# Weight sums on GpSimd in steps of 128 columns, and two blocks of attention outputs half a position later, in a fused attention and gated feed-forward kernel

## The chip, the cores and the metric

The kernel runs on one core of a Trainium2 chip. The metric is the device time of one execution in microseconds (us): before the change the median of three runs is 1006.04 us (1006.01 to 1006.66). Engines are named as in the profile: PE is TensorE, with PEld its weight loads; DVE is VectorE, ACT is ScalarE, POOL is GpSimd, and SP the queue that issues the DMAs.

## The reference

Windowed causal attention over 8 batches, 8 heads, 576 positions and head width 64, followed by a gated feed-forward layer over all 4608 tokens:

```
scores = q @ k.T / sqrt(64), kept where 0 <= i - j < 64
attn   = softmax(scores);  x = attn @ v, as (4608, 512)
gate   = sigmoid(x @ w_gate)          # 512 x 1536
val    = x @ w_val                    # 512 x 1536
out    = (gate * val) @ w_out         # 1536 x 512
```

q, k and v are float32; the three weight matrices come as float64 and are converted on the chip.

## The kernel before, in words

**Tiles.** The tokens are cut into twelve tiles of 384 (TT). The attention of a tile is done in four units (t, p), p being a pair of heads. The feed-forward layer runs over pairs of tiles, s = 0 to 5. Every product of full precision is made from a high and a low part of each operand: x_hi w_hi + x_lo w_hi + x_hi w_lo. A tile "hi" is a rounded copy made by ACT or DVE, and "lo" is the difference, made by DVE or POOL (split, line 145).

**A unit** goes through stages. stage_a or stage_s (lines 194, 263) makes the scores on PE (L208) into two PSUM banks and the softmax: DVE adds the mask and finds the minimum (L232), ACT takes the exponential and its sum (L241), DVE inverts the sums (L249, L250), and DVE or POOL multiplies by the inverse (L259). stage_b (line 285) transposes the probabilities on PE (L290), and ACT copies each half to SBUF as pT (L295). stage_c (line 300) multiplies by v on PE (outputs, L319), into a bank oo, and ACT copies it to xf (L307). From the third tile on, scores, transposes and outputs all take their banks from one pool of two (a_bank, line 191), in turn: two for the scores, two for the transposes, one for the outputs. The second bank of a unit's scores is therefore the one that the outputs of the unit before held.

**The first pair** (s = 0) uses plain products, up (L349) and down (L419), while weights are still being converted: conv_a on ACT (L112, L113), conv_b on DVE (L121 to L125), conv_c on ACT and DVE (L146, L147), with stores and loads on SP. The attention of the second pair's tiles (the third and fourth tile) runs in between.

**The later pairs** use a scheme of Strassen's kind: seven products in place of eight (product, L568, in PRODUCTS order), for each of k = 0 to 5 and for gate and value (m = 0, 1). It needs sums of quarters of the weights, S1 to S4. These sums are made once, during the first two pairs, twelve sets (m, k) in all, and stored to DRAM for the pairs behind. The functions are:

- sums_load (line 477) loads the two weight blocks a1 and a2.
- sums_make (line 492) makes four sums of 128x256 on POOL (L496 to L499) in a tile sw.
- sums_split (line 502) takes the hi part of two sums at once, 128x512, on ACT (L146), and the lo part on POOL (L147), in tiles ws.
- sums_store (line 514) stores the parts on SP (L471), one DMA for each sum.

In the second pair DVE combines the products from PSUM (u and c, L574; the copy p, L580), multiplies by the gate (h, L608; hb, L613), and makes hl (L388). PE's next product into a bank waits for these readers.

**Order.** Every step is put at a time in planner units (put, line 623), and the events are traced in order of time. PE's instructions keep exactly that order (pe, line 83). The order on the other engines is dealt by the framework's scheduler, which plays the program through with its own instruction times. The plan of the first pair is a list: items up (0, j), down (0, j-1), up (1, j) for j = 0 to 11. Line 661 says at which positions of that list the stages a, b and c of the eight units of the third and fourth tile stand. A whole number is ahead of that item; a half is between the gate product and the value product of an up item (attend, line 666). Units go in the order of unit(1, n), so that n = 0 and 1 are the first two units of the third tile.

Of the kernel before, what the change touches and what calls it, by code (L numbers as in the profile page):

```python
# [9 lines left out]
F32 = mybir.dt.float32  # L10
# [8 lines left out]
P = 128  # L19
# [7 lines left out]
def attn_ffn(ctx: ExitStack, tc: tile.TileContext, qT, kT, vN, w_gate, w_val, w_out, out):  # L27
# [3 lines left out]
    nc = tc.nc  # L31
# [95 lines left out]
    def conv_c(i):  # L127
        j, m = divmod(i, KINDS)
        _, w32 = conv.pop(i)
        H = DM // 2  # L130
        tag, bufs = ("W", WB) if m < 2 else (f"wo_{j}", 1)
        w2 = wts.tile([P, 2, 2, H], F32R, name=f"w{m}_{j}", tag=tag, bufs=bufs)
        if m == 2:
# [11 lines left out]
    def split(w32, hi, lo, eng):  # L145
        cp = nc.scalar.copy(hi, w32)  # L146
        eng.tensor_sub(out=lo, in0=w32, in1=hi.bitcast(F32))  # L147
        return cp.ins
# [341 lines left out]
        sums[m, k] = aa  # L490

    def sums_make(m, k):
        H = DM // 2
        a1, a2 = sums[m, k]
        sw = mp.tile([P, 4, H], F32, name=f"sw_{m}_{k}", tag="raw", bufs=RAW)
        nc.gpsimd.tensor_add(out=sw[:, 0, :], in0=a2[:, :H], in1=a2[:, H:])  # L496
        nc.gpsimd.tensor_sub(out=sw[:, 1, :], in0=sw[:, 0, :], in1=a1[:, :H])
        nc.gpsimd.tensor_sub(out=sw[:, 2, :], in0=a1[:, :H], in1=a2[:, :H])
        nc.gpsimd.tensor_sub(out=sw[:, 3, :], in0=a1[:, H:], in1=sw[:, 1, :])  # L499
        sums[m, k] = sw  # L500

    def sums_split(m, k):

        H = DM // 2
        sw, sums[m, k] = sums[m, k], []
        for i in range(0, 4, 2):
            w2 = wts.tile([P, 2, 2, H], F32R, name=f"ws{i}_{m}_{k}", tag="W", bufs=WB)
            split(sw[:, i:i + 2, :], w2[:, :, 0, :], w2[:, :, 1, :], nc.gpsimd)
            sums[m, k].append(w2)
            for e in range(2):  # L510
                n = [w for w, _, _ in PRODUCTS].index(f"S{i + e + 1}")
                wt[(1, k, m, n)] = w2[:, e]
# [136 lines left out]
    def unit(s, n):  # L649
        return 2 * s + n // 2 % 2, n // 4 + n % 2 * 2  # L650
# [7 lines left out]
        if n < NF:  # L658
            plan.append(("up", 1, n))
    at, now = {}, 0.0  # L660
    for n, at_plan in enumerate(((4.5, 8, 8.5), (9, 12, 13), (13.5, 16, 17), (17.5, 20.5, 22),
                                 (22.5, 25, 26), (26.5, 30, 31), (31.5, 35, 36), (36.5, 40, 41))):
        for f, x in enumerate(at_plan):
            fill.setdefault(x, []).append((f, *unit(1, n)))
# [64 lines left out]
    for s in range(1, NS):  # L729
# [17 lines left out]
        for k in range(NK):  # L747
            if s == 1:
                for m in range(2):
                    for d, f in ((-6, sums_load), (0, sums_make), (7, sums_split), (11, sums_store)):  # L750
                        put(now - (21 if k else 38) + 13 * m + d, 7, f, m, k)
                for x, d in enumerate((-18, -14, -5)):
                    put(now + d, 7.5, a_load, s, k, x)
            else:
                for q in range(NPR):
                    put(now - 24 + 3 * q, 7.5, w_load, s, k, q)
            for m in range(2):
                for n in range(NPR):
                    put(now, 9, product, s, k, m, n)
                    now += PRT  # L760
                    if n in (2, 4, 6) and len(downs) > (RESERVE if m else 0) * (k == 1):
                        j, x = downs.pop(0)
                        put(now, 9, down, a, j, x, j == 0, False)
                        now += DPT
                    attend(slot)
                    slot += 1
            downs += [(j, x) for j in (k, k + NK) for x in range(TB)]
# [65 lines left out]
```

## Time and profile before

| | |
|---|---|
| median of 3 runs | 1006.04 us |
| the profiled execution's own time | 1005.49 us |
| its span | 1003.2 us |
| granted PE clock, mean | 0.998 |
| PE busy | 978.2 us (98%) |
| DVE, ACT, POOL busy | 641.8, 530.8, 231.5 us |

The span is the time from the first instruction to the last in one execution that the hardware profiler took; the 2.3 us more in that execution's own time lie around it. Busy times count instructions of the engine, without queue waits. In lists of instructions, the first number is the start in us from the span's start and the second the duration; what stands in brackets is the engine's idle time just ahead and the instruction that ended it. In lists of waits, the numbers are us in total, times, and the longest. In lists by tile, they are the minimum, median and maximum of the duration in ns. In groups by line, they are busy us, mean ns of one, and idle us ahead.

### The profile page before, as it was taken

How to read it: one execution, taken by the hardware profiler on the slowest of the kernel's cores; microseconds unless marked ns; L12 is line 12 of the kernel's file. 1: busy time of each engine (PE TensorE's matmuls, PEld its weight loads, DVE VectorE, ACT ScalarE, POOL GpSimd, SP SyncE). 2: the span in 40 equal slices, each digit the busy share in tenths (PEclk: the TensorE clock that was granted, in tenths of full speed). 3: DMA queues.
4: the chain of work that ended last, by engine and by line, in shares of the span. 5: the costliest groups of instructions: out<-in, count | busy, mean ns of one | idle time of the engine just before them, and what ended most of it. 6: DMA issues, size and time to landing. Idle time of an engine off the chain costs nothing.

```text
span 1003.2 us, 19702 instructions
## 1 busy us (share of the span) xinstructions
PE 978.2 (98%) x6984; PEld 881.6 (88%) x6984; DVE 641.8 (64%) x1737; ACT 530.8 (53%) x1433; POOL 231.5 (23%) x240
## 2 busy tenths in 40 slices
PE   6999999999999999999999999999999999999998
PEld 5888999889888889999988999988999988999996
DVE  7899888636766665666675666575666667344532
ACT  7887878544655745545554555464564464211122
POOL 4200122225454031212141121213212124010100
PEclk9999999999999999999999999999999999999999
DMA  9999888469875625767643776751776661566500
GB/s 345 315 340 363 319 287 274 157 233 298 256 246 187 219 77 177 246 207 227 216 136 97 236 235 203 224 184 45 241 236 215 202 184 71 159 214 204 189 32 32
DMA packets 84337, 208.91 MB, mean 208 GB/s; under 512 B 9360, under 2 KB 24976, under 8 KB 84240
## 3 DMA queue, kind: packets, MB, share of 16 engines
q1 hardware_dynamic: 84240, 207.66, 63.0%
q8 instruction: 56, 0.92, 0.4%
q14 instruction: 41, 0.34, 0.1%
HBM read 165.94 MB, written 41.68 MB: 207 GB/s over the span
## 4 chain that ended last, share of the span: by engine, by line
PE 64%; ACT 4%; DVE 1%; issue 0%; DVEq 0%; ACTq 0%
PE pr L568 35%; PE y L419 23%; PE s L208 2%; ACT p L241 2%; PE pp L290 2%; PE s L319 1%; ACT g L362 1%; ACT e L361 0%; PE pr L319 0%; PE oo L319 0%; DVE u L574 0%; ACT L241 0%; DVE rs L249 0%; DVE c L574 0%; DVE g L366 0%
## 5 line engine op out<-in xcount | busy, mean ns | idle before, releaser
L419 PE MATMUL y<-w,hh 128*128 128x512 f32 x804 | 250.3, 392 | 0.0
L568 PE MATMUL pr<-x_T,wt 128*128 128x384 f32 x1152 | 226.4, 338 | 0.5
L568 PEld LDWEIGHTS pr<-x_T,wt 128*128 128x128 f32 x1152 | 202.3, 188 | 11.0 <-DVE u L574 4.2
L568 PE MATMUL pr<-x_B,wt 128*128 128x384 f32 x864 | 176.4, 340 | 0.1
L419 PEld LDWEIGHTS y<-w,hh 128*128 128x128 f32 x804 | 148.2, 188 | 21.5 <-ACT hh L384 1.4
L419 PE MATMUL y<-w,hl 128*128 128x512 f32 x402 | 158.4, 394 | 0.0
L568 PEld LDWEIGHTS pr<-x_B,wt 128*128 128x128 f32 x864 | 150.6, 188 | 8.3 <-issue 2.6
L574 DVE TENSOR_TENSOR u<-pr,p 128x384 f32<-128x384 f32 x120 | 66.5, 554 | 138.7 <-PE pr L568 138.3
L259 POOL TENSOR_TENSOR p<-p,rs 128x384 f32<-128x384 f32 x76 | 65.4, 874 | 289.0 <-DVE rs L250 230.2
L241 ACT ACTIVATE p<-p,mn 128x128 f32<-128x128 f32 x288 | 111.1, 393 | 26.9 <-DVE mn L232 26.1
L388 POOL TENSOR_TENSOR hl<-h,hh 128x384 fp32r<-128x384 f32 x48 | 50.0, 1041 | 283.9 <-DVE hh L386 283.9
L349 PE MATMUL ph<-x,w 128*128 128x384 f32 x576 | 106.6, 339 | 0.5 <-ACT g L372 0.5
L349 PEld LDWEIGHTS ph<-x,w 128*128 128x128 f32 x576 | 99.5, 188 | 2.8 <-issue 1.0
L419 PEld LDWEIGHTS y<-w,hl 128*128 128x128 f32 x402 | 75.3, 187 | 18.1 <-DVE hl L388 1.9
L232 DVE CUSTOM_DVE_ANT_0 p<-s,m 128x128 f32<-128x128 f32 x288 | 66.2, 286 | 20.2 <-PE s L208 20.2
L574 DVE TENSOR_TENSOR c<-pr,u 128x384 f32<-128x384 f32 x120 | 66.7, 556 | 10.9 <-ACT g L372 5.7
L388 DVE TENSOR_TENSOR hl<-hb,hh 128x384 fp32r<-128x384 f32 x60 | 39.1, 663 | 41.4 <-ACT hh L384 41.0
L295 ACT COPY pT<-pp 128x384 f32<-128x384 f32 x96 | 41.7, 482 | 42.8 <-PE pp L290 42.4
L582 ACT COPY p<-pr 128x384 f32<-128x384 f32 x48 | 22.6, 471 | 68.4 <-PE pr L568 67.8
L384 ACT CAST hh<-hb 128x384 fp32r<-128x384 f32 x60 | 30.0, 512 | 51.4 <-PE y L419 51.3
L208 PE MATMUL s<-k,q 64*64 64x128 f32 x1152 | 46.3, 290 | 7.4 <-DMA k<-in_kT_dram 5.7
L574 DVE TENSOR_TENSOR c<-pr,p 128x384 f32<-128x384 f32 x60 | 33.4, 557 | 28.8 <-PE pr L568 27.8
(95 smaller groups left out, 1406.3 us busy)
## 6 DMA issues: line engine op xcount, KB each, us to landing
wt<-wd SPq DMA_DIRECT2D x168, 512.0 KB, 4.1
v<-in_vN_dram SPq DMA_DIRECT2D x48, 384.0 KB, 4.5
wd<-ws SPq DMA_DIRECT2D x48, 256.0 KB, 3.4
k<-in_kT_dram SPq DMA_DIRECT2D x48, 224.0 KB, 4.7
q<-in_qT_dram SPq DMA_DIRECT2D x48, 192.0 KB, 4.2
wd<-w SPq DMA_DIRECT2D x36, 256.0 KB, 6.1
wa<-wd SPq DMA_DIRECT2D x36, 256.0 KB, 4.1
out_dram<-yo SPq DMA_DIRECT2D x33, 256.0 KB, 2.0
```

The costliest lines, as they stand in the source:

```text
L208: pe(nc.tensor.matmul(sc[h][half * BLK:(half + 1) * BLK, u, :], qt[h * BLK:(h + 1) * BLK, U * BLK:(U + 1) * BLK], kt[h * BLK:(h + 1) * BLK ...
L232: nc.vector.tensor_tensor_reduce(out=pt[:, u, :], in0=sc[:, u, :], in1=masks[key], op0=ALU.add, op1=ALU.min, scale=-SCALE, scalar=3.0e38, ...
L241: exp = nc.scalar.activation(pt[:, u, :], pt[:, u, :], AF.Exp, bias=mn[:, u:u + 1], scale=-1.0, **sums)
L259: eng.tensor_mul(out=pt, in0=pt, in1=rs.unsqueeze(2).broadcast_to([P, UP, P]))
L295: cp = nc.scalar.copy(pT, pp)
L349: pe(nc.tensor.matmul(ph, l, r, start=i == 0, stop=i == len(prs) - 1))
L384: nc.scalar.copy(h_hi, h32)
L388: return eng.tensor_sub(out=h_lo, in0=h32, in1=h_hi.bitcast(F32))
L419: pe(nc.tensor.matmul(yb[y], l, r, start=first and n == 0, stop=last and n == 2))
L568: pe(nc.tensor.matmul(ps, l, r, start=new and i == 0, stop=i == len(prs) - 1, skip_group_check=not new))
L574: nc.vector.tensor_add(out=o, in0=ps, in1=a)
L582: nc.scalar.copy(tmp["p1"], ps)
```

## The change

sums_make works in steps of 128 columns: each of its four operations on 256 columns becomes two on 128, first both steps of one operation, then both of the next. sums_split calls ACT's copy itself, unchanged at 128x512, and makes the lo part in four subtractions on POOL of 128 columns, two for each sum, in place of one of 512. A set of sums is now made by sixteen POOL instructions in place of six. Data, tiles, casts and stores are the same.

In line 661, stage_c of the first two units of the third tile goes from position 8.5 to 9 and from 13 to 13.5. Before, the first block of outputs stood between the gate and the value product of up (0, 3); now it stands behind that value product, ahead of down (0, 2), and directly ahead of the scores of the second unit, whose stage_a is at 9. The second stood ahead of the gate product of up (1, 4); now it stands behind that product, directly ahead of the scores of the third unit at 13.5.

```diff
     def sums_make(m, k):
         ...
-        nc.gpsimd.tensor_add(out=sw[:, 0, :], in0=a2[:, :H], in1=a2[:, H:])
-        nc.gpsimd.tensor_sub(out=sw[:, 1, :], in0=sw[:, 0, :], in1=a1[:, :H])
-        nc.gpsimd.tensor_sub(out=sw[:, 2, :], in0=a1[:, :H], in1=a2[:, :H])
-        nc.gpsimd.tensor_sub(out=sw[:, 3, :], in0=a1[:, H:], in1=sw[:, 1, :])
+        lo, up = ([slice(h + c, h + c + P) for c in range(0, H, P)] for h in (0, H))
+        for c, d in zip(lo, up):
+            nc.gpsimd.tensor_add(out=sw[:, 0, c], in0=a2[:, c], in1=a2[:, d])
+        for c in lo:
+            nc.gpsimd.tensor_sub(out=sw[:, 1, c], in0=sw[:, 0, c], in1=a1[:, c])
+        for c in lo:
+            nc.gpsimd.tensor_sub(out=sw[:, 2, c], in0=a1[:, c], in1=a2[:, c])
+        for c, d in zip(lo, up):
+            nc.gpsimd.tensor_sub(out=sw[:, 3, c], in0=a1[:, d], in1=sw[:, 1, c])
         sums[m, k] = sw
 
     def sums_split(m, k):
         ...
-            split(sw[:, i:i + 2, :], w2[:, :, 0, :], w2[:, :, 1, :], nc.gpsimd)
+            nc.scalar.copy(w2[:, :, 0, :], sw[:, i:i + 2, :])
+            for e in range(2):
+                for c in range(0, H, P):
+                    cs = slice(c, c + P)
+                    nc.gpsimd.tensor_sub(out=w2[:, e, 1, cs], in0=sw[:, i + e, cs],
+                                         in1=w2[:, e, 0, cs].bitcast(F32))
             sums[m, k].append(w2)
         ...
-    for n, at_plan in enumerate(((4.5, 8, 8.5), (9, 12, 13), (13.5, 16, 17), (17.5, 20.5, 22),
+    for n, at_plan in enumerate(((4.5, 8, 9), (9, 12, 13.5), (13.5, 16, 17), (17.5, 20.5, 22),
```

## The prediction

> **What bounds the kernel now.** I read the page first, then the busy times by stretch, TensorE's waits in the stretches that the change touches, and at last the timeline around each of these waits.
>
> ```profile
> span 1003.2 us, 19702 instructions
> PE 978.2 (98%) x6984; PEld 881.6 (88%) x6984; DVE 641.8 (64%) x1737; ACT 530.8 (53%) x1433; POOL 231.5 (23%) x240
> ```
>
> TensorE (PE) is busy for 978 of 1003 us; only its 25 us of idle time can be won. The busy times by stretch (us, then PE, PEld, DVE, ACT, POOL) show where they lie:
>
> ```profile
> 215.00:351.00 136.00, 129.78 (x997) 117.96 (x996) 86.63 (x224) 78.97 (x200) 56.39 (x56) 1.00 0.75 240
> 383.00:511.00 128.00, 127.80 (x1016) 118.45 (x1015) 83.97 (x258) 70.54 (x226) 24.83 (x27) 1.00 0.71 222
> ```
>
> The products of the second pair of tiles (215 to 351 us) leave PE idle for 6.2 us, those of the third pair for 0.2. What differs is GpSimd (POOL), which makes the weight sums there: 56 us against 25. PE's waits in that stretch:
>
> ```profile
> PE pr L568 <- DVE u L574: 3.4, 5, 0.7
> PE pr L568 <- DVE c L574: 1.3, 2, 0.6
> PE pr L568 <- ACT g L372: 0.9, 1, 0.9
> PE pp L290 <- DVE p L259: 0.7, 1, 0.7
> ```
>
> 5.4 of these 6.3 us name VectorE (DVE). The timeline says why DVE is late; one of four like it is at 271 to 273 us, below another instance of the same DVE instruction:
>
> ```profile
> 259.85 0.19 DVE L249 SCALAR_TENSOR_TENSOR rs<-rs 128x6 f32<-128x6 f32 x1 [1.01 <-ACT p L241]
> ...
> 271.19 1.30 POOL L147 TENSOR_TENSOR ws<-sw,ws 128x512 fp32r<-128x512 f32 x1 [4.35 <-DMA v<-in_vN_dram]
> 271.55 0.97 DVE L249 SCALAR_TENSOR_TENSOR rs<-rs 128x6 f32<-128x6 f32 x1 [1.22 <-ACT p L241]
> ...
> 272.65 0.52 DVE L574 TENSOR_TENSOR u<-pr,p 128x384 f32<-128x384 f32 x1
> 273.22 0.97 PE L568 MATMUL pr<-x_T,ws 128*128 128x384 f32 x4 [0.71 <-DVE u L574]
> ```
>
> The tiny DVE instruction on rs starts inside POOL's 512-column subtraction and ends 0.03 us after it: 0.97 us where the one at 259.85 took 0.19. DVE behaves as if locked out until POOL's instruction ends. Which DVE work is hit, the groups of DVE in this stage show:
>
> ```profile
> L608 DVE TENSOR_TENSOR h<-c,g 128x384 f32<-128x384 f32 x6 | 5.3, 880 | 0.2
> L608 DVE TENSOR_TENSOR h<-pr,g 128x384 f32<-128x384 f32 x6 | 3.3, 552 | 0.0
> ```
>
> One line and one size: 880 ns with both inputs in SBUF, 552 with one in PSUM (pr). So POOL's instruction blocks SBUF-fed DVE work for its whole length.
>
> **Part 1, the GpSimd steps.** Removed per set of sums: four instructions of 256 columns and two of 512; added: sixteen of 128. Minimum, median and maximum of the present ones (ns):
>
> ```profile
> L147 POOL TENSOR_TENSOR ws<-sw,ws x24: 1274/1298/2271, 161.2 to 329.4; 128x512 fp32r<-128x512 f32 x24
> L496 POOL TENSOR_TENSOR sw<-a x12: 724/739/2872, 145.8 to 308.1; 128x256 f32<-128x256 f32 x12
> ```
>
> By the medians a column costs (1298-739)/256 = 2.18 ns, so a 128-column step takes 739-280 = 0.46 us, an estimate. A set goes from 4x0.739+2x1.298 = 5.55 to 16x0.46 = 7.36 us; twelve sets add 21.7 us of POOL time. No PE wait names POOL, and the sums stand well ahead of use: the set split at 329.4 is still being used at 345 to 350. I cost the added time itself at nothing. Two queues wait for POOL. ScalarE's casts come later by up to 1.8 us a set, and ACT is busy for only 79 of these 136 us. On SP the stores of the sums wait, with loads of q, k, v and weights queued behind them:
>
> ```profile
> SPq L471 <- POOL ws L147: 32.0, 17, 4.7
> ```
>
> They will wait up to 1.8 us a set longer. PE's four waits above name no DMA, so the loads' lead covers that; where it didn't, a set would cost up to those 1.8 us.
>
> The Trainium skill (GPSIMD Engine Reference, Elementwise) puts a two-input operation at about 2.6 cycles a column, near this slope, but 4497 ns for 2048 columns, which leaves some 60 ns of fixed cost, so about 0.34 us a step; the rows give 0.18 us of fixed cost and decide. With the page's step POOL's added time would vanish, and DVE at the sites (a) below would find POOL done (0.34 against 0.36 us), which makes the sum 0.3 larger.
>
> What counts is how long DVE is shut out: at most one step of 0.46 us, not 0.74 or 1.30. By sites:
>
> (a) The four waits at 273.22, 295.62, 308.76 and 331.46 are 3.4 less the 0.49 of this one, which has no POOL instruction near it and stays:
>
> ```profile
> 344.21 1.32 PE L568 MATMUL pr<-x_T,ws 128*128 128x384 f32 x6 [0.49 <-DVE u L574]
> ```
>
> So 2.9 us. DVE's rs starts 0.36 us after POOL; the first small step ends 0.46 after it, leaving 0.1 of waiting instead of 0.78. u comes 0.68 earlier, 0.65 of each wait goes: 2.6. Bounds: a whole step each time leaves 0.32x4 = 1.3; no wait gives 2.9.
>
> (b) The two waits on c (1.3 us) have the same history. The second:
>
> ```profile
> 252.62 1.59 POOL L147 TENSOR_TENSOR ws<-sw,ws 128x512 fp32r<-128x512 f32 x1 [3.64 <-ACT ws L146]
> 253.11 1.52 DVE L608 TENSOR_TENSOR h<-c,g 128x384 f32<-128x384 f32 x1
> ...
> 255.18 0.74 POOL L496 TENSOR_TENSOR sw<-a 128x256 f32<-128x256 f32 x1
> 255.26 1.08 DVE L388 TENSOR_TENSOR hl<-h,hh 128x384 fp32r<-128x384 f32 x1
> 255.88 1.06 POOL L498 TENSOR_TENSOR sw<-a,a 128x256 f32<-128x256 f32 x1
> 257.50 0.80 PE L568 MATMUL pr<-x_T,ws 128*128 128x384 f32 x3 [0.65 <-DVE c L574]
> ```
>
> Two blocked instructions lose 0.97 and 0.53 us against 0.55, 1.5 in all; two whole steps lose 0.92. DVE is 0.6 earlier at least, which takes the 0.65 away: 1.2 for both. One more collision in the chain leaves 0.15 each: 0.3 to 1.3.
>
> (c) Before the second pair, PE waits for normalized probabilities behind POOL:
>
> ```profile
> 193.33 1.09 DVE L540 TENSOR_TENSOR t<-xf,t 128x384 f32<-128x384 f32 x1
> ...
> 195.62 1.44 DVE L259 TENSOR_TENSOR p<-p,rs 128x384 f32<-128x384 f32 x1
> ...
> 197.20 0.52 PE L290 MATMUL pp<-ident,p 128*128 128x128 f32 x3 [0.79 <-DVE p L259]
> ```
>
> Excess 0.54 and 0.89, 1.43; two steps would be 0.92. That frees 0.5 at least, 0.79 at most: 0.6.
>
> (d) The wait for p inside the stage (0.7 us):
>
> ```profile
> 260.30 1.29 DVE L259 TENSOR_TENSOR p<-p,rs 128x384 f32<-128x384 f32 x2
> ...
> 342.66 1.03 DVE L259 TENSOR_TENSOR p<-p,rs 128x384 f32<-128x384 f32 x2
> ```
>
> Only 0.26 of it is contention; with a step of 0.46 in the way, -0.2 to +0.26: 0.1. The wait on ACT's gate (0.9) is none of POOL's: 0.
>
> Against this, 21.7 us more of POOL activity in some 190 us raise the chance of a collision by a ninth. The groups of DVE by line hold about 110 instructions there of the kinds seen blocked (among them hl 19, p 20, x 19, hb 11); 12 more collisions at half a step are 2.8 us of DVE, whose load is 64%: 0.5 to PE, bounds 0 and 1.5.
>
> Sum of part 1: 2.6+1.2+0.6+0.1-0.5 = 4.0 us gained. Bounds: 1.3+0.3+0.5-0.2-1.5 = 0.4 and 2.9+1.3+0.8+0.3 = 5.3.
>
> **Part 2, the outputs.** Two blocks of 24 small matmuls are moved behind one more product of 12. They issue no DMA, and no queue but PE's and ACT's order is touched. Removed are two waits, at 71.27 and 91.20:
>
> ```profile
> 71.27 1.29 PE L319 MATMUL oo<-pT,v 128*64 128x64 f32 x24 [0.91 <-ACT pT L295]
> 72.49 2.37 PE L349 MATMUL ph<-x,w 128*128 128x384 f32 x12
> 74.79 0.89 PE L208 MATMUL s<-k,q 64*64 64x128 f32 x24
> ...
> 91.20 1.29 PE L319 MATMUL oo<-pT,v 128*64 128x64 f32 x24 [1.41 <-ACT pT L295]
> ```
>
> Both blocks also stretch to 1.29 us against 0.92 undisturbed (below), as the second half's copy comes late. So 0.91+0.37 = 1.28 and 1.41+0.37 = 1.78 us. The product now ahead of them takes 2.3 us (72.49 to 74.79): both copies are then done.
>
> Added is a wait. Until now that product stood between the outputs and the next unit's scores. Now the scores follow directly, and their second bank is the one that the outputs fill and ACT must first copy away. In-order PE then stands still with all products behind it. The nearest rows have just that order:
>
> ```profile
> 185.30 0.92 PE L319 MATMUL oo<-pT,v 128*64 128x64 f32 x24
> ...
> 186.79 0.88 PE L208 MATMUL s<-k,q 64*64 64x128 f32 x22 [0.22 <-ACT xf L307]
> ```
>
> From 185.30 to 187.67 are 2.37 us, against 0.92+0.89 = 1.81: 0.56 lost when ACT is free. Here it isn't:
>
> ```profile
> 74.21 0.47 ACT L307 COPY xf<-oo 128x384 f32<-128x384 f32 x1
> ...
> 77.38 0.68 ACT L112 ACTIVATE w<-raw 128x512 f32<-128x512 f32 x1 [0.80 <-DMA w32d<-w]
> ...
> 93.17 0.46 ACT L307 COPY xf<-oo 128x384 f32<-128x384 f32 x1
> ```
>
> The copies started 1.65 us after their outputs' end (72.56) and 0.68 (92.49). If ACT keeps its order: the first unit's outputs could now begin at 71.27-0.91+2.3 = 72.7 and end at 73.6; the copy is done at 74.7, so 1.1 is lost for 1.28. The second's begin at 91.20-1.41+2.3 = 92.1 and end at 93.0, the copy at 93.6: 0.7 with its latency, lost for 1.78. The first unit's balance hardly matters, for a later wait absorbs up to 0.5 of it either way:
>
> ```profile
> 84.72 2.36 PE L349 MATMUL ph<-x,w 128*128 128x384 f32 x12 [0.50 <-ACT g L372]
> ```
>
> That gate comes from ACT, which at 77.38 stood behind a DMA, not behind PE. Part 2: 0 and +1.1; I take 0.6, since ACT's weight conversion, on which the later gates hang, can claim half back. Bounds per unit: gains of 1.28 and 1.78 less 0.56 at best; at worst a copy 2 us behind its outputs costs 2.5: -1.2+0.5-0.7 = -1.4 (the 0.5 being what that wait absorbs). At best 0.5+1.2 = 1.7.
>
> **Sum.** 4.0+0.6 = 4.6 us off the profiled execution's 1005.49 (span 1003.2 and 2.3 around it) gives 1000.9. That execution lies 0.55 below the median of 1006.04, so the median should be 1001.4.
>
> **Rivals.** (1) The outputs lose: 1.4 us for the copies' sake. ACT was 1.65 us late once, which speaks for it; part 1 still brings 4.0: 1003.4.
>
> (2) The win on POOL is taken by the next thing in DVE's queue. The wait at 344.21 has no POOL near it and is still 0.49: after the softmax sums DVE is simply late with u. If the planner, which times POOL differently now, re-deals ACT's and DVE's order so that sites (a) end like that one, they yield 0.2 each, 0.9, with (b) 0.3, (c) 0.5, (d) 0 and 0.5 against: 1.2, and nothing from part 2: 1004.8. For it: both queues are dealt by that planner. Against: only POOL's costs change in it there.
>
> (3) Slower: the lock is not handed to DVE between POOL's steps; a run of steps keeps it. At (a) rs would wait for four steps, 1.84 us instead of 1.30: 0.5 each, 2.2. At (b), h loses 0.5 and hl, now behind eight steps of 3.68 instead of one of 0.74, some 1 to 2.9 more: about 2 each. With (c) that is near 7 less what DVE's slack takes, some 4 us: 1010. It decides from three steps on (1.38 against 1.30). Against it: at 255.88 POOL, with work queued, let DVE's hl go first and itself took 1.06. The Trainium skill (SBUF — State Buffer, two separate sides) states an exclusive lock for the whole instruction, given to whoever starts first; it promises DVE no turn between back-to-back instructions. The hand-over at 255.88 is this trace's answer, on one boundary.
>
> That the change does nothing would need the small steps to be joined again; no row shows such a thing.
>
> **How the numbers follow.** 0.2%, 2 us, is about what a measurement of this kernel can tell from no change. Forecast 0.62: 1001.4, its own range 999.0 (5.3+1.7 gained) to 1003.4. Rival 1 0.12: 1003.4, still faster. Rival 2 0.16: 1004.8, within 0.2%. Rival 3 0.10: slower. Faster is 0.62+0.12 = 0.74, same 0.16, slower 0.10. The range from 999.0 to 1005.8 (a microsecond beyond rival 2) leaves out rival 3 and little of the others.
>
> **What would show it.** Right: POOL instructions of about 0.46 us; rs and h<-c,g near 0.3 and 0.7 us in the second pair; PE's waits on u and c there under 2 us in all; the waits on pT at 71 and 91 gone, waits of scores on xf of 0.3 to 1 us in their place. Wrong: DVE waits spanning several POOL steps, PE waits on ACT's casts or on ws, or scores waiting over 2 us for xf.

## The result and the profile after

The changed kernel takes 999.38 us (median of 8 runs, 999.0 to 1004.09) against 1005.94 for the kernel before beside it: a ratio of 0.994, interval 0.993 to 0.995, so 0.6% faster. The forecast was 1001.4 with a range of 999.0 to 1005.8, so the result lies 0.4 us inside the range's fast end.

The page of the changed kernel, span and busy times:

```profile
span 997.6 us, 19847 instructions
PE 979.2 (98%) x6984; PEld 884.1 (89%) x6984; DVE 633.0 (63%) x1737; ACT 530.5 (53%) x1433; POOL 253.5 (25%) x360
```

POOL is busy for 22 us more, as the estimate of the steps had it (21.7), and the span is 5.6 us shorter. Its instructions by tile (minimum, median, maximum in ns):

```profile
L518 POOL TENSOR_TENSOR ws<-sw,ws x96: 453/466/1446, 160.9 to 325.2; 128x128 fp32r<-128x128 f32 x96
L499 POOL TENSOR_TENSOR sw<-a x24: 452/462/2597, 145.4 to 305.1; 128x128 f32<-128x128 f32 x24
```

A step takes 0.46 us, as worked out. PE's waits between 200 and 352 us:

```profile
PE pp L290 <- DVE p L259: 1.0, 3, 0.6
PE pr L579 <- ACT g L372: 0.9, 1, 0.9
PE pr L579 <- DVE u L585: 0.5, 1, 0.5
```

The waits on c are gone, and of those on u one of 0.49 is left, the one without POOL. The site that the prediction showed at 271 to 273 us, DVE first and then POOL:

```profile
268.94 0.17 DVE L249 SCALAR_TENSOR_TENSOR rs<-rs 128x6 f32<-128x6 f32 x1 [1.22 <-ACT p L241]
269.14 0.19 DVE L250 RECIPROCAL rs<-rs 128x6 f32<-128x6 f32 x1
269.25 0.52 DVE L585 TENSOR_TENSOR u<-pr,p 128x384 f32<-128x384 f32 x1
```

```profile
268.59 2.04 POOL L518 TENSOR_TENSOR ws<-sw,ws 128x128 fp32r<-128x128 f32 x4 [3.91 <-ACT ws L514]
```

rs starts 0.35 us into POOL's run of four steps, as before, and takes 0.17 us instead of 0.97. The first step ends at 269.05, 0.11 us behind the start of rs, so what is left of it to wait for is less than the 0.17 us that rs takes anyway. It is POOL that pays: four steps of 0.46, 1.84 in sum, take 2.04. The groups of DVE in this stage:

```profile
L619 DVE TENSOR_TENSOR h<-c,g 128x384 f32<-128x384 f32 x6 | 3.6, 604 | 0.2
L619 DVE TENSOR_TENSOR h<-pr,g 128x384 f32<-128x384 f32 x6 | 3.3, 553 | 0.0
```

The SBUF-fed form has come down from 880 to 604 ns; the PSUM-fed one is as it was.

Where the time came from, two landmarks tell: the transposes at which the stage begins and those near its end. Before, they started at 195.92 and 332.62 us; now:

```profile
195.56 0.82 PE L290 MATMUL pp<-ident,p 128*128 128x128 f32 x6
...
326.30 0.49 PE L290 MATMUL pp<-ident,p 128*128 128x128 f32 x3
```

Between them lay 136.70 us and lie now 130.74: 5.96 us won there. Ahead of them this execution is 0.36 us earlier, and behind them 0.7 us of it all is lost again up to the end. In that early part, the wait that was forecast has come, and is long (PE first, then ACT):

```profile
72.59 0.92 PE L319 MATMUL oo<-pT,v 128*64 128x64 f32 x24
73.44 0.43 PE L208 MATMUL s<-k,q 64*64 64x128 f32 x2
75.79 1.25 PE L208 MATMUL s<-k,q 64*64 64x128 f32 x22 [1.92 <-ACT xf L307]
76.97 1.22 PE L419 MATMUL y<-w,hh 128*128 128x512 f32 x2
```

```profile
73.21 1.25 ACT L113 ACTIVATE raw<-raw 128x512 int32<-128x512 uint32 x2
74.71 0.68 ACT L113 ACTIVATE raw<-raw 128x512 int32<-128x512 uint32 x1 [0.26 <-DMA raw<-in_moe_w_out_dram]
75.29 0.45 ACT L307 COPY xf<-oo 128x384 f32<-128x384 f32 x1
```

Before, the copy stood ahead of that third conversion, which waited for the same DMA behind it:

```profile
74.21 0.47 ACT L307 COPY xf<-oo 128x384 f32<-128x384 f32 x1
75.39 0.69 ACT L113 ACTIVATE raw<-raw 128x512 int32<-128x512 uint32 x1 [0.70 <-DMA raw<-in_moe_w_out_dram]
```

With the outputs moved, ACT has the conversion first, and the copy begins at 75.29 instead of 74.21.

After the wait PE is slow: 1.22 us for a pair that took 0.73 before. The busy times by stretch show the granted clock (the column behind PE's) at half:

```profile
74.00:76.00 2.00, 0.21 (x8) 1.00 1.04 409
76.00:78.00 2.00, 2.00 (x25) 0.54 1.04 391
78.00:80.00 2.00, 2.00 (x7) 0.61 1.17 353
80.00:82.00 2.00, 2.00 (x13) 1.00 0.89 225
```

### The profile page after: what moved, and what is told of

Read it like the earlier page. It is cut to its first block, busy times and chain, and to the rows that moved or that the text cites. A ratio compares the mean times of both kernels' runs of the same rounds, so it can differ in the third digit from the quotient of the medians.

```text
span 997.6 us, 19847 instructions
## 1 busy us (share of the span) xinstructions
PE 979.2 (98%) x6984; PEld 884.1 (89%) x6984; DVE 633.0 (63%) x1737; ACT 530.5 (53%) x1433; POOL 253.5 (25%) x360
## 4 chain that ended last, share of the span: by engine, by line
PE 84%; ACT 6%; DVE 4%; DMA 2%; issue 1%; DVEq 0%; ACTq 0%; SPq 0%
PE pr L579 40%; PE y L419 29%; PE ph L349 7%; PE s L208 3%; ACT p L241 3%; PE pp L290 3%; DMA w32d<-w 1%; PE s L319 1%; PE oo L319 1%; ACT g L362 1%; ACT e L361 1%; DVE p L232 1%; DMA wd<-w 1%; PE pr L319 1%; DVE u L585 0%
## 5 line engine op out<-in xcount | busy, mean ns | idle before, releaser
L518 POOL TENSOR_TENSOR ws<-sw,ws 128x128 fp32r<-128x128 f32 x96 | 50.1, 556 | 36.2 <-ACT ws L514 30.7
```

Of the source, the lines that this page charges most:

```text
L518: nc.gpsimd.tensor_sub(out=w2[:, e, 1, cs], in0=sw[:, i + e, cs], in1=w2[:, e, 0, cs].bitcast(F32))
```

## The experiments

The theory: DVE's SBUF-fed instructions are shut out until the end of the POOL instruction that they run into; the shorter POOL instructions of the second pair are the gain, and the moved outputs are worth little. The rivals: the moves carry half of it; the planner dealt another order. The stage column is the time between the two landmarks above, from each run's profile.

| run | POOL: sums / lo part | outputs | ratio to before (interval) | median us | stage us |
|---|---|---|---|---|---|
| before | 256 / 512 | 8.5, 13 | 1 | 1005.1 to 1006.2 | 136.70 |
| changed | 128 / 128 | 9, 13.5 | 0.994 (0.993 to 0.995) | 999.38 | 130.74 |
| steps_only | 128 / 128 | 8.5, 13 | 0.9944 (0.9932 to 0.9955) | 999.81 | 130.40 |
| moves_only | 256 / 512 | 9, 13.5 | 1.0012 (1.0001 to 1.0024) | 1006.8 | 136.70 |
| make_only | 128 / 512 | 8.5, 13 | 1.0004 (0.9991 to 1.0018) | 1007.21 | 137.37 |
| lo_256 | 128 / 256 | 8.5, 13 | 0.9945 (0.993 to 0.9961) | 1000.38 | 133.06 |
| lo_only | 256 / 128 | 8.5, 13 | 0.9936 (0.9923 to 0.9948) | 999.11 | 130.67 |
| lo_64 | 128 / 64 | 8.5, 13 | 0.9936 (0.9923 to 0.9949) | 999.76 | 130.84 |

### The two parts apart

steps_only takes the changed kernel and puts the outputs back:

```diff
-    ...(((4.5, 8, 9), (9, 12, 13.5), ...
+    ...(((4.5, 8, 8.5), (9, 12, 13), ...
```

> Only the GpSimd steps of 128 columns; the outputs stand where they stood before. Theory (GpSimd shuts DVE out for the length of one instruction, and shorter instructions are the whole gain): PE, DVE and ACT issue in the very order of the kernel before, PE's waits on u and c in the second pair fall from 4.7 us to about 0.5, rs (L249) from 574 to about 220 ns, and the median is about 1000.3 us, 5.6 below before. Rival (the moved outputs carry half the gain or more): 1003 us or above.

Measured: 0.9944 of before, which is the changed kernel's ratio. In its trace PE, DVE and ACT have the very order of the kernel before, so the planner re-dealt nothing. PE's waits between 200 and 350 us are those of the changed kernel, and rs takes 182 ns on the average:

```profile
L249 DVE SCALAR_TENSOR_TENSOR rs<-rs 128x6 f32<-128x6 f32 x8 | 1.5, 182 | 10.0 <-ACT p L241 10.0
```

moves_only is the converse: the kernel before with the two positions of the change.

> Only the two blocks of outputs moved; GpSimd works in 256 and 512 columns as before. Theory: the first move loses (scores wait for xf by about 1.9 us near 74 us, and the granted PE clock falls to about 0.55 for 4 us behind that), the second wins about as much and a little more; median about 1005.3 us, waits on u and c in the second pair stay at 4.7 us. Rival (the moves are worth 2 us or more): 1004 us or below.

Measured: 1.0012 of before, with an interval of 1.0001 to 1.0024: no gain, and if anything a small loss; the stage is unchanged to 0.01 us. The rival of 2 us or more falls. The changed kernel itself, run again beside the kernels below:

> The changed kernel itself, beside the others of this call. Steps alone gave 0.9944 of before and the changed kernel 0.994. If the moves are worth nothing on the average, it comes out at 0.994 to 0.996 again; if they win 0.6 us as forecast, at 0.9938. PE waits near 74 us for scores on xf by 1.5 to 2.2 us in any case, and the clock falls behind that.

It came to 0.9945 (0.9931 to 0.9959), and its scores waited 2.04 us for xf. With and without the moves the ratio is the same. A gain of 0.6 us could hide in these two intervals; that of moves_only leaves no room for it.

### Which steps, and which size

make_only splits the four sums and leaves the lo part in one instruction of 512 columns; lo_only does the opposite.

```diff
+ make_only: sums_make as in the change, sums_split as before
+ lo_only:   sums_make as before, sums_split as in the change
```

> Outputs as before the change; only the making of the sums in steps of 128, the lo part in one instruction of 512 as before. Theory (the lo part's 1.30 us cause the four waits on u and most of the two on c): waits on u stay near 3.4 us, rs near 570 ns, the waits on c 0.3 to 1.3 us; median 1004 to 1005 us. Rival (both halves carry it alike): waits on u and c fall to half, 1002.5 us.

> Outputs as before the change; the lo part in steps of 128, the sums still made in four instructions of 256. Theory: the four waits on u go (0.5 us left in all), since the lo part caused them; the two waits on c lose the larger half of their cause (h behind the lo part) but not hl behind the sums: 0 to 0.2 us each; median 1001 us. Rival (the make steps carry the gain): 1003 us or more, with the waits on u at 3 us.

Measured: make_only wins nothing. PE's waits in its second pair (timeline of PE, those on DVE but for one of 0.21 us behind the second and the last of 0.49):

```profile
241.95 1.31 PE L573 MATMUL pr<-x_T,wa 128*128 128x384 f32 x6 [1.34 <-DVE u L579]
262.20 0.52 PE L290 MATMUL pp<-ident,p 128*128 128x128 f32 x3 [1.97 <-DVE p L259]
...
274.42 1.32 PE L573 MATMUL pr<-x_T,ws 128*128 128x384 f32 x6 [0.72 <-DVE u L579]
296.81 1.32 PE L573 MATMUL pr<-x_T,ws 128*128 128x384 f32 x6 [0.72 <-DVE u L579]
309.82 1.32 PE L573 MATMUL pr<-x_T,ws 128*128 128x384 f32 x6 [0.72 <-DVE u L579]
332.22 1.32 PE L573 MATMUL pr<-x_T,ws 128*128 128x384 f32 x6 [0.72 <-DVE u L579]
```

The four waits (a) stand as before. The two on c went, but waits of 1.34 and 1.97 us came: with longer making, a 512-column instruction of 1.61 us fell upon the two normalizations p at 239.31, which took 2.12 us, and likewise at 260.38. lo_only has the whole gain, with the waits of the changed kernel (0.5 on u, none on c, 1.0 on p). The expectation that hl behind the 256-column sums would still cost 0 to 0.2 us at each wait on c came out at 0. So the lo part is the gain, and the sums need not have been split.

lo_256 has the lo part in steps of 256, lo_64 in steps of 64:

```diff
-                for c in range(0, H, P):
-                    cs = slice(c, c + P)
+                for c in range(0, H, H):            # lo_64: range(0, H, P // 2)
+                    cs = slice(c, c + H)            # lo_64: c + P // 2
```

> Outputs as before the change; the sums made in steps of 128, but the lo part in steps of 256 (0.74 us each), two for each sum pair. Theory (DVE is shut out until the end of the GpSimd instruction it runs into): at the four sites rs starts 0.36 us into a step that now ends at 0.74, so rs takes 0.4 to 0.6 us, and PE's waits on u there are about 0.3 us each, 1.7 us in all with the one of 0.49 that stays; median 1001.5 us. Rival (any split at all is enough, since GpSimd lets DVE in at boundaries that come at 0.46 us only by chance): waits on u of 0.5 in all and 1000 us.

> Outputs as before the change; sums in steps of 128, the lo part in steps of 64, eight for each sum pair, about 0.32 us each by the slope of 2.18 ns a column. Theory (DVE waits for the rest of one step, and nothing of PE's waits on DVE is left to win below 128): waits on u 0.5 us in all, rs about 0.2 us, median 1000 us as with steps of 128, though GpSimd is busy for 30 us more. Rival (every step costs DVE a hand-over, or late sums are felt): PE waits on ws, casts or DVE by 1 us more, 1001 us or above.

In lo_256 the site of the prediction's example looks so, DVE and then PE:

```profile
270.29 0.41 DVE L249 SCALAR_TENSOR_TENSOR rs<-rs 128x6 f32<-128x6 f32 x1 [1.21 <-ACT p L241]
```

```profile
271.41 1.34 PE L579 MATMUL pr<-x_T,ws 128*128 128x384 f32 x6 [0.15 <-DVE u L585]
293.24 1.32 PE L579 MATMUL pr<-x_T,ws 128*128 128x384 f32 x6 [0.15 <-DVE u L585]
305.64 1.31 PE L579 MATMUL pr<-x_T,ws 128*128 128x384 f32 x6 [0.15 <-DVE u L585]
```

This is the dose at the sites (a): rs takes 0.97, 0.41 and 0.17 us for lo steps of 512, 256 and 128 columns, and PE's wait is 0.71 (0.72 in make_only), 0.15 and 0. PE, DVE and ACT have the same order of instructions in all of them; only the length and the number of POOL's instructions differ. At the fourth site of lo_256 no wait is left at all; its 1.7 us on u, which equal the expectation, are made up by a new wait of 0.74 at 240.64, where steps of 256 columns had delayed rs (0.65 us) and the normalizations p. PE's waits on p came to 1.4 us there, against 1.0 in steps_only. The waits were half of the 0.3 us expected, since the blocked instruction took 0.41, not its 0.19 and the rest of the step on top. By the stage lo_256 is 2.7 us behind steps_only; its timed runs don't show that (0.9945 against 0.9944). Its profiled execution had no fall of the clock at all, the other profiles between one and four, each worth some 1.7 us (see the last section): the first hundred microseconds scatter by as much as what was to be told apart here. The rival that any split does is refuted by the stage and the waits, not by the times.

lo_64 wins nothing more. Its POOL instructions, by tile, and PE's waits:

```profile
L518 POOL TENSOR_TENSOR ws<-sw,ws x192: 310/322/1295, 162.2 to 327.8; 128x64 fp32r<-128x64 f32 x192
```

```profile
PE pp L290 <- DVE p L259: 1.2, 3, 0.8
PE pr L579 <- ACT g L372: 0.9, 1, 0.9
PE pr L579 <- DVE u L585: 0.5, 1, 0.5
```

POOL is busy for 15 us more than in the changed kernel (268.9 against 253.5), and nothing waits for it: neither hand-overs nor late sums are felt. The site of the prediction's example, POOL and then DVE:

```profile
269.61 2.92 POOL L518 TENSOR_TENSOR ws<-sw,ws 128x64 fp32r<-128x64 f32 x8 [2.71 <-ACT ws L514]
```

```profile
269.96 0.28 DVE L249 SCALAR_TENSOR_TENSOR rs<-rs 128x6 f32<-128x6 f32 x1 [1.22 <-ACT p L241]
```

rs again starts 0.35 us into POOL's run. Here that is 0.07 us into the second step, which runs from 269.89 to 270.21, and rs ends at 270.24, while six steps of the run follow. So DVE is let in at the end of the step, and the part of the step that is left counts: 0.25 us at 64 columns, but 0.11 at 128. That 128 columns left no wait at all at the sites (a) is partly a matter of where rs falls.

### The outputs

second_move keeps only the second of the two moves; scores_later keeps both and sets the second unit's scores behind down (0, 2), at position 10.

```diff
+ second_move:  ...(((4.5, 8, 8.5), (9, 12, 13.5), ...
+ scores_later: ...(((4.5, 8, 9), (10, 12, 13.5), ...
```

> The changed kernel with the first unit's outputs put back to 8.5; the second stays at 13.5. Theory (the first move is a loss): no wait on xf near 74 us and no fall of the clock, the old wait of 0.9 us on pT near 70 us is back, and the median is about 998.3 us, 1 below the changed kernel. Rival (the weight conversion on ACT and DVE sets the pace there, and a later wait on a gate takes back what is won): 999.4 us, as the changed kernel.

> The changed kernel with the second unit's scores at position 10 in place of 9, so that the nine matmuls of down (0, 2) stand between the first unit's outputs and them. Theory (the loss of the first move is only the missing cover for the copy to xf): the wait on xf near 74 us shrinks from 1.9 to 0.3 us or less, no fall of the clock, median about 998 us. Rival (scores 2 us later make the second unit's softmax late, and PE waits at its transposes or for the gate behind the exponentials): 999.4 us or more.

Both expectations were missed. second_move has a median of 1002.03 us (0.9963, 0.9949 to 0.9976), slower than the changed kernel's, though the interval touches that of changed_again. In its profile, of an execution of 1004.59 us, the move that I took for the winning one waits as long as the other did, PE first and ACT behind it:

```profile
98.96 1.55 PE L208 MATMUL s<-k,q 64*64 64x128 f32 x22 [2.10 <-ACT xf L307]
```

```profile
97.91 0.62 ACT L146 CAST w<-w 128x512 fp32r<-128x512 f32 x1 [1.40 <-DVE w L125]
98.44 0.47 ACT L307 COPY xf<-oo 128x384 f32<-128x384 f32 x1
```

The copy stands behind a cast that waits 1.40 us for DVE. That is not the rule: the same scores waited 0.26 us in the profiles of the changed kernel, changed_again and moves_only. scores_later takes 1000.71 us (0.9954, 0.9942 to 0.9966): its wait on xf near 74 us is gone, and 2.14 us of waiting for the gate at 86.64, with a fall of the clock, have come in its place, the rival's case.

copies_first leaves the outputs where they were before the change, keeps the steps, and ties two conversions and a cast on ACT behind the copies pT in front of which they stood:

```diff
+        with tc.issue_after(marks[("copy", 2, 0)]) if i in (11, 13) else nullcontext():   # conv_a, first activation
+                if f is conv_c and a[0] == 14:
+                    behind.enter_context(tc.issue_after(marks[("copy", 2, 2)]))
```

> The GpSimd steps, outputs as before the change, and an order edge on ACT: the copies pT of the two units go ahead of the two conversions (and of one cast) that stood in front of them and waited for a DMA or for DVE. Theory (the waits at 71 and 91 us were ACT's in-order queue, not the place of the outputs): both waits on pT fall below 0.3 us, no fall of the clock there, median about 997.5 us, 2 below the steps alone. Rival (the weight conversion sets the pace of this stage, so that the time comes back as a wait on the gate near 84 us or on casts): 999.5 us.

Measured: 0.9937 (0.9924 to 0.995), 999.44 us, not to be told from steps_only. Against the 997.5 us that the theory expected, that is a miss. The wait on pT at 71 us is gone, one of 0.3 at 90 is left, and there is no fall of the clock after 60 us. (The planner dealt DVE's order anew between 71 and 104 us, too.) The outputs start at 70.34 instead of 71.27, but PE reaches the gate no sooner:

```profile
74.73 0.88 PE L209 MATMUL s<-k,q 64*64 64x128 f32 x22 [0.82 <-ACT xf L309]
...
84.68 2.36 PE L351 MATMUL ph<-x,w 128*128 128x384 f32 x12 [0.53 <-ACT g L374]
```

Before the change this product started at 84.72 after a wait of 0.50, so the gate takes back next to nothing. What was won at 71 us is given back at 74.7, where the scores wait 0.82 us for xf: ACT's copy starts at 74.21 as it did before, because a cast ahead of it in ACT's queue waits for DVE's conversion until 72.17 (72.18 before). That fits the rival's cause, the weight conversion that sets the pace, but the time came back at another wait than those it named. Behind the second unit 0.6 us remain (transposes at 103.54 against 104.13 in steps_only).

lo_and_copies joins lo_only and copies_first:

```diff
+ sums_make as before, sums_split as in the change, outputs at 8.5 and 13, order edges as in copies_first
```

> The lo part in steps of 128, the sums in four instructions of 256, outputs as before the change, and ACT's copies pT ahead of the conversions. Theory (the lo part is the whole gain of the steps, and the copies are worth about 0.6 us on the average): median 999 us, 0.993 of before, no fall of the clock between 60 and 110 us. Rival (the copies are worth nothing on the average): 999.7 us.

It is the fastest by its median, 998.6 us (998.17 to 998.92), 0.9928 (0.9916 to 0.994), and its clock doesn't fall after 60 us. Its interval touches those of steps_only and lo_only, so that it beats the changed kernel is likely and not shown.

## Why the prediction was right, point by point

**The bound and the cause.** Right: in the second pair PE's order was unchanged, and what was won there was time that PE lost to waits for DVE, behind POOL's long instructions. steps_only and lo_only, in which PE, DVE and ACT have the order of the kernel before, and the dose of 512, 256 and 128 columns show it. That the number came out inside the range is in part luck: part 1 won more than its upper bound, part 2 won nothing, and the range's fast end of 999.0 held only because it had 1.7 us for part 2 in it.

**(a)** 2.6 us forecast; the four waits of 2.9 us vanished whole, since rs at 268.94 took 0.17 us and no wait shows in it, where 0.1 was put. **(b)** 1.2 forecast, 1.3 gone. **(c)** 0.6 forecast, all 0.79 gone: at 195.56 the six transposes follow each other without a wait. **(d)** +0.1 forecast; one wait on p of 0.68 became three of 0.63, 0.21 and 0.18 us, a loss of 0.3. **New collisions**, 0.5 set against the gain: beside (d) PE shows one. At 237.35 rs runs into a step and takes 0.46 us (0.19 before), u comes late, and PE has lost 0.4 us by the product at 239.89.

**The mis-sized term** of part 1 is what a wait costs beside its idle time. Between the two landmarks the waits of PE fell from 6.5 us (those of the prediction's sites and ACT's 0.9) to 1.7 (0.88, 0.63 and 0.21), by 4.8; the stage became 5.96 us shorter. The seven waits that vanished, (a), (b) and (c), had 4.95 us of idle time and returned 6.0, some 0.15 more each. Where PE does not wait, its rows overlap, here in the kernel before:

```profile
276.14 1.22 PE L568 MATMUL pr<-x_T,wa 128*128 128x384 f32 x6
277.20 1.20 PE L568 MATMUL pr<-x_B,ws 128*128 128x384 f32 x6
```

The first ends at 277.36, 0.16 us after the second has started. A wait takes that overlap away as well, and the idle time does not count it; the sum counted idle time only. At the sites (a) the product behind the vanished wait starts 0.8 us sooner for 0.71 of idle time. Part 1 was thus 5.6 us by the ratio of steps_only and 6.0 (6.3 in steps_only) by the stage, and not 4.0, above its upper bound of 5.3.

**Part 2**, 0.6 us forecast, was not confirmed: moves_only is no gain, and the changed kernel equals steps_only. The mechanism, a wait on xf for one on pT, was right; the step that failed is the condition "if ACT keeps its order", on which the 1.1 us lost behind the first outputs rested. ACT's order changed: the conversion that waits for a DMA went ahead of the copy, which began 1.1 us later than before. 1.92 us of waiting came, with a fall of the clock worth 1.7 on top. It was over 2 us in two other profiles (2.04 in changed_again, 2.17 in moves_only), which the prediction had named as a sign of being wrong. In this profile the first move, put at 0, cost 1.8 us up to the transposes of the second unit (88.67 against 86.91); the second, put at 1.1, won 1.4 back (104.38 against 104.00). DVE's order was dealt anew as well, though the prediction had only PE's and ACT's touched.

But the old positions can lose as much: steps_only waited 2.14 us for pT in its profile, where the kernel before, with the same order, had 0.91; the conversion ahead of the copy waited 1.14 us for its DMA there, and 0.57 before. These waits hang on what ACT's conversions and casts wait for, a DMA or DVE, and that differs from one execution to the next. What each move is worth by itself stays open within about 1 us. That a later gate absorbs part of the first unit's balance was right: the wait of 0.50 at 84.72 is gone in the changed kernel.

**The rivals.** That the lock is kept over a run of steps (1010 us) is refuted by rs in lo_256 and lo_64, which ends 0.02 to 0.03 us behind the step that it ran into while the run goes on, and by the times. The Trainium skill (SBUF — State Buffer, two separate sides) states an exclusive lock for the whole instruction: the dose agrees with it, and these runs add that DVE got its turn at the next boundary within a run. The re-dealt planner's order is refuted for the steps, which left the order of PE, DVE and ACT as it was; for the moves the order of ACT and DVE did change. Not tested is where in a run of steps DVE's instruction falls: it is the same 0.35 us at the sites (a) of all these kernels.

## What to carry to other kernels

Where GpSimd and VectorE work side by side, look for VectorE instructions with all inputs in SBUF that end just after a GpSimd instruction: their excess is the price of GpSimd's longest instruction, and cutting that one, not the others, returned it here, at the cost of GpSimd time that was idle anyway. Cut until the remaining wait has cover; below that there was nothing more to win here. Then read the engine's waits over the whole stage again, since steps of another length fall upon other work. PE's wait for a copy on a busy ACT was not cured by moving the consumer: ask what stands in front of the copy, whether the planner keeps it there, and what waits for it next.

## What the runs showed of the hardware that was not expected

Between 60 and 110 us PE's granted clock fell to half after waits of 1.5 to 2.2 us, in the changed kernel after 1.92, in steps_only after 2.14, in lo_only after 1.54. In the changed kernel the clock of the four microseconds from 76 us was 0.58, 0.50, 0.50 and 0.71, so it was missing 1.71 us in all, or 3.4 us at half speed. The length of one wait does not decide it: 2.00 us of waiting in lo_256, 1.97 in make_only and 1.41 in the kernel before passed without a fall, and the changed kernel's other fall, from 21 to 25 us, stands behind two waits of only 0.74 and 0.75. What decides it stays open. The Trainium skill (TensorE: Matmul & The Clock Gate, what's actually happening) has a free-running window of about 3.4 us and half the clock after at least one idle window. The length of the low phase agrees; the single waits ahead of the falls here were shorter than one window.
